# A state-space convolution beside a feed-forward block: late tiles transposed by VectorE, a three-row power table, the response's transform moved behind the next pair's run, and later marks

## The chip, the cores and the metric

The kernel runs on one core of a Trainium2 chip. The metric is device time in microseconds for one execution, lower is better. Engines are named as in the profile: PE is TensorE's matrix multiply, PEld its weight load, DVE is VectorE, ACT is ScalarE, POOL is GpSimd, SP is SyncE (here it only issues transfers). L-numbers are lines of the kernel before.

## The reference

All in float32, for one sequence of 2048 positions and 576 channels:

```python
x = A_u
xn = _layernorm(x, axis=-1)
return x + _A_ref(xn, ...) + _B_ref(xn, B_w1, B_w2)
```

`_B_ref` is the feed-forward block (FFN): `silu(xn @ w1) @ w2`, with 4608 hidden columns. `_A_ref` is a long convolution along the positions, one response per channel:

```python
dt = jnp.exp(log_dt)[:, None]
logdA, dB = dt * (A_re + 1j * A_im), dt * (B_re + 1j * B_im)
P = jnp.exp(logdA[:, :, None] * l[None, None, :])
K = jnp.einsum("dn,dnl,dn->dl", Cc, P, dB).real
...
y = irfft(rfft(pad(u)) * rfft(pad(K)))[:L] + u * Dskip
```

The response K of a channel is a sum over 128 states, at 2048 lags; generating it and the two transforms is what runs beside the FFN.

## The kernel before

**The main line of work** is the FFN (`ffn`). Positions are cut into 16 tiles of 128, four tiles make a block of 512, two blocks a half. For each half and each of nine chunks of hidden columns (four times 128), both blocks are worked on: `up` (L276) makes 128 hidden columns for 512 positions, 14 matmuls of 512 columns into `ph`; ACT applies silu (`gf`, L292) and rounds it to 12 bits (`gh`, L293), DVE takes the rest (`gl`, L294). `down` (L296) multiplies back, 24 matmuls of 288 columns for a tile into `po` (L309), and DVE adds to `acc` (L313). Every float32 operand is split in a high and a low part, and three products stand for one, so weights too are split when they arrive: w1r into w1h and w1l, w2r into w2h and w2l (L245 to L274). SP issues the weight loads.

**What is woven in** is a generator, `side` (L753). `weave` (L31) traces the FFN step by step (144 steps) and advances `side` when its next yield, a share of the FFN, has come; `marks = (0.13, 0.595, 0.822)` (L755) are the shares at which generation begins, the spectral stage begins, and that stage ends. From this trace a scheduler makes the fixed order in which each engine runs its instructions. `behind(x)` pins instructions after x on x's engine.

In order, `side` does this:

- `phase0` (L197) loads x, normalizes tiles in pairs (`norm`), and `put_xt` (L117) turns each tile on PE: four transposes of 128 by 128 into `pt` (L121), rounded by ACT into xh (L122), the rest by DVE into xl (L123), then the last 64 channels (L125 to L127). Tiles 0 to 7 go straight into the operands `xts` of the first half. Tiles 8 to 15 (the late tiles) are turned in the same way into `xt` and stored to `dxt`, both parts, in runs of 128 columns (L223); `next_xt` (L320) fetches xh, xl and x4 from there on POOL's queue when the last chunk of the first half begins. `dxn` keeps the normalized rows for the convolution.
- `natural` (L373) computes, per state and channel, the response's magnitude and phase and decay powers: `ex` holds the decay for 256, 64, 8 and 1 lags (L422), stored to `dexp`; `turned` (L387) transposes on PE into rhoT (magnitude) and phiT (phase).
- `kgen` (L490) generates the response in 36 runs of 16 channels, two runs to a pair. `load_bases` brings the decay bases of a pair, `powers` (L524) raises them to powers 0 to 7 in `pw`, four rows for a channel, and multiplies row 1 by rhoT into `al` (L536). Each run forms a phase table (`th`, `c65`; sines on ACT), a magnitude table in C (`al` times row 0, L562; row 2 times row 3, L566), and from them S and C (L577, L578). After the second run 64 small matmuls sum over the states into `kp` (L598), ACT copies it to `kt` (L605), eight matmuls with f1 (L613) make the first transform `z`, and ACT moves z into `stage` (L621), which every second pair SP stores to d1k (L626). The matmuls `pu` between them (L152, L153) are the same transform of the input (`spread`). kp, z, pu, pt and the spectral stage's pk and pb take turns in three PSUM banks (`pss`); po has three of its own (`ps2`), ph two.
- `spectral` (L632) works through 32 frequencies: loads, splits, products, the inverse of the inner transform into `pb`, ACT's copy `yo`, stored by POOL to d2 (L672).
- `tail` (L677) and the last chunk's `down` load d2 back as `ys` (L728; `conv_load`), and `add_conv` (L731) does the outer inverse in eight small matmuls `py` (L741) for a tile, added by DVE (L747). A ys needs all 32 frequencies.

Two things about the tile shapes matter: kp's matmuls use the array in strips of 32 columns (`tile_position=(0, 32 * q)`), z's in halves of 64 rows, py's in 64 by 32; all FFN matmuls use the whole array.

## Time and profile before

| | |
|---|---|
| median of 3 runs (lowest to highest) | 1133.25 us (1133.01 to 1133.71) |
| the profiled execution's own time | 1131.89 us |
| its span in the profile | 1130.1 us |
| PE busy, PEld busy | 1109.0 us, 999.9 us |
| DVE busy, ACT busy, POOL busy | 917.1, 709.0, 74.3 us |
| DVE busy from 180 to 660 us (generation) | 457.8 of 480 us |
| granted TensorE clock | 1.00 in all stretches up to 1110 us |
| bytes moved | 151.24 MB, 134 GB/s |

The span is the profile's, from the first to the last instruction; the execution's own time has 1.8 us more around it. A row of a group tells line, engine, operation, output and inputs, shape, count, then busy time and the mean of one in ns, then the engine's idle time just before it and what ended that. A row of the timeline gives start and length in us; PE's instructions overlap, so the length of one is not its price, and the step from start to start is. The ends of matmuls are modelled.

### The profile page before, as it was taken

To read this page: it belongs to the slowest core of one execution; us is meant where nothing else is said; L and a number is where in the kernel's file an instruction comes from. 1 tells how busy PE (TensorE), PEld (TensorE's weight loads), DVE (VectorE), ACT (ScalarE), POOL (GpSimd) and SP (SyncE) were. 2 spreads that over 40 slices of the span, in tenths; PEclk is the share of its full clock that TensorE was granted. 3 is DMA by queue.
4 is the path that set the end of the run, shared out by engine and by line. 5 is a ranking of instruction groups with operands and counts; after the bars stand their busy time and mean duration, and the time that the engine had idled before them with its cause. 6 is when DMAs were issued, how large, how long until landed. Compare 5 with 4: busy or idle time off the path is not lost.

```text
span 1130.1 us, 22882 instructions
## 1 busy us (share of the span) xinstructions
PE 1109.0 (98%) x9184; PEld 999.9 (88%) x9184; DVE 917.1 (81%) x1540; ACT 709.0 (63%) x1235; POOL 74.3 (7%) x130
## 2 busy tenths in 40 slices
PE   6999999999999999999999999999999999999998
PEld 5988889988889888898989999999999999998876
DVE  6699779999999999999999937788877878763433
ACT  4665355776777666667666637877777787752211
POOL 1010000000000000001000000000000000000210
PEclk9999999999999999999999999999999999999999
DMA  9345431334241424255954264554535536239661
GB/s 277 111 142 181 144 96 60 97 98 103 83 114 59 112 83 106 90 127 192 231 161 104 66 183 122 157 175 132 170 114 157 166 118 195 72 111 243 174 171 55
DMA packets 160458, 151.24 MB, mean 134 GB/s; under 512 B 87216, under 2 KB 127168, under 8 KB 159712
## 3 DMA queue, kind: packets, MB, share of 16 engines
q1 hardware_dynamic: 150128, 112.66, 36.2%
q0 software_dynamic: 9840, 36.24, 10.0%
q8 instruction: 72, 1.18, 0.4%
q10 hardware_dynamic: 384, 0.89, 0.3%
q14 instruction: 34, 0.28, 0.1%
HBM read 103.74 MB, written 46.08 MB: 133 GB/s over the span
## 4 chain that ended last, share of the span: by engine, by line
PE 65%; DVE 24%; DMA 5%; ACT 3%; issue 3%; POOL 0%; SPq 0%; DVEq 0%; ACTq 0%; POOLq 0%
PE po L309 28%; PE ph L284 23%; DVE acc L313 2%; DVE C L566 2%; PE pu L721 2%; PE pb L721 2%; PE pk L721 2%; DVE th L541 2%; DMA w2r<-in_B_w_dram 2%; DVE th L558 2%; DVE S L577 2%; PE ph L285 2%; PE ph L286 2%; DVE C L577 2%; DVE gl L294 2%
## 5 line engine op out<-in xcount | busy, mean ns | idle before, releaser
L309 PE MATMUL po<-w2h,gh 128*128 128x288 f32 x1152 | 338.5, 297 | 5.3 <-DVE acc L313 2.6
L309 PE MATMUL po<-w2l,gh 128*128 128x288 f32 x1152 | 337.1, 295 | 0.0
L309 PE MATMUL po<-w2h,gl 128*128 128x288 f32 x1152 | 335.3, 296 | 0.6 <-DVE gl L294 0.6
L309 PEld LDWEIGHTS po<-w2h,gh 128*128 128x128 f32 x1152 | 215.2, 188 | 16.8 <-DVE acc L313 4.9
L309 PEld LDWEIGHTS po<-w2l,gh 128*128 128x128 f32 x1152 | 215.5, 188 | 4.3
L309 PEld LDWEIGHTS po<-w2h,gl 128*128 128x128 f32 x1152 | 214.8, 188 | 3.0 <-issue 0.9
L284 PE MATMUL ph<-xh,w1h 128*128 128x512 f32 (+1 forms) x592 | 162.3, 390 | 0.5 <-ACT xh L122 0.5
L284 PE MATMUL ph<-xl,w1h 128*128 128x512 f32 (+1 forms) x592 | 162.1, 387 | 0.0
L284 PE MATMUL ph<-xh,w1l 128*128 128x512 f32 (+1 forms) x592 | 161.1, 385 | 0.0
L313 DVE TENSOR_TENSOR acc<-po,acc 128x288 f32<-128x288 f32 x288 | 126.9, 452 | 40.1 <-PE po L309 38.4
L292 ACT ACTIVATE gf<-ph 128x512 f32<-128x512 f32 (+1 forms) x148 | 86.6, 585 | 115.3 <-PE ph L286 106.1
L294 DVE TENSOR_TENSOR gl<-gf,gh 128x512 fp32r<-128x512 f32 (+1 forms) x148 | 99.6, 673 | 47.6 <-ACT gh L293 46.9
L284 PEld LDWEIGHTS ph<-xl,w1h 128*128 128x128 f32 x592 | 108.6, 190 | 20.2
L284 PEld LDWEIGHTS ph<-xh,w1l 128*128 128x128 f32 x592 | 108.0, 188 | 19.7
L284 PEld LDWEIGHTS ph<-xh,w1h 128*128 128x128 f32 x592 | 105.3, 190 | 19.0 <-issue 2.3
L293 ACT CAST gh<-gf 128x512 fp32r<-128x512 f32 (+1 forms) x148 | 89.7, 608 | 9.1 <-PE po L309 6.2
L559 ACT ACTIVATE c<-th 128x1040 f32<-128x1040 f32 x36 | 38.7, 1075 | 60.0 <-DVE th L558 59.9
L271 ACT CAST w2h<-w2r 128x576 fp32r<-128x576 f32 x72 | 46.7, 672 | 39.9 <-DMA w2r<-in_B_w_dram 23.4
L557 ACT ACTIVATE c<-th,magic 128x1040 f32<-128x1040 f32 x36 | 42.0, 1168 | 42.4 <-DVE C L578 36.5
L273 DVE TENSOR_TENSOR w2l<-w2r,w2h 128x576 fp32r<-128x576 f32 x72 | 53.4, 752 | 8.9 <-ACT w2h L271 8.9
L286 PE MATMUL ph<-x,w1l 128*128 128x512 f32 (+1 forms) x148 | 56.9, 385 | 0.0
L255 DVE TENSOR_TENSOR w1l<-w1r,w1h 128x640 fp32r<-128x640 f32 x72 | 56.7, 819 | 0.2
(186 smaller groups left out, 1847.2 us busy)
## 6 DMA issues: line engine op xcount, KB each, us to landing
w2r<-in_B_w_dram SPq DMA_DIRECT2D x72, 288.0 KB, 3.7
w1r<-in_B_w_dram SPq DMA_DIRECT2D x35, 512.0 KB, 3.8
d1u<-u POOLq DMA_DIRECT2D x32, 288.0 KB, 2.8
d1k<-stage SPq DMA_DIRECT2D x18, 512.0 KB, 7.2
ur<-d1u SPq DMA_DIRECT2D x32, 288.0 KB, 3.6
kr<-d1k SPq DMA_DIRECT2D x32, 288.0 KB, 2.8
d<-yo POOLq DMA_DIRECT2D x32, 288.0 KB, 3.6
ys<-d SPq DMA_DIRECT2D x32, 288.0 KB, 9.0
```

The lines of the kernel that those rows point to most:

```text
L255: pins["w1l"] = nc.vector.tensor_sub(l1, src, h1).ins
L271: pins["w2h"] = nc.scalar.copy(h2, r2).ins
L273: nc.vector.tensor_sub(l2, r2, h2)
L284: nc.tensor.matmul(ph, w[:, kt, :], v[:, kt, a:e], start=n + kt == 0, stop=False)
L286: pins["pe"] = nc.tensor.matmul(ph, l1[:, 4, :], x4[:, a:e], start=False, stop=True).ins
L292: nc.scalar.activation(gf, ph, AF.Silu)
L293: pins["gh"] = nc.scalar.copy(gh, gf).ins
L294: pins["gl"] = nc.vector.tensor_sub(gl, gf, gh).ins
L309: pins["pe"] = nc.tensor.matmul(po[:, :HD], G[blk, t][g][:, js], W2[half, c, t][w][:, hs], start=n == 0, stop=n == 3 * FT - 1).ins
L313: nc.vector.tensor_add(acc[j][:, hs], po[:, :HD], acc[j][:, hs])
L577: nc.vector.tensor_mul(ov3, t[:, :, 0:64].rearrange("n d (x y) -> n d x y", y=32), mv3)
L721: nc.tensor.matmul(dst, st, mv[:, hs], start=n == 0, stop=n == 3 * len(terms) - 1)
```

## The change

It has five parts, which touch each other little.

- **Late tiles turned by DVE.** For tiles 8 to 15 `put_xt` is no longer called. DVE's transpose, which turns each 32 by 32 block in place, is applied to the normalized tile as a whole, once for a tile, and eight transfers on SP for a pair put the blocks where they belong in a plain float32 `dxt` of 576 by 512, in runs of 32 columns (128 bytes). `next_xt` fetches the plain values into xl's place and the last 64 channels twice into a `gl` buffer, and the new `split_xt` rounds (ACT) and subtracts (DVE), 128 channels at a time, after the steps d3, u1 and u2 of the last chunk's blocks in the first half.
- **Three-row power table.** The decay for 64 lags leaves `ex`'s interleaved part and is kept apart; `pw` has three rows for a channel instead of four. The magnitude times its four powers of the 64-lag decay is computed once in `natural` (`wt`, three products of 576 columns), stored to `dmag`, and loaded for each pair as `wb` beside `eb`. The products `al` go, and the first magnitude product is done in two halves.
- **Transform behind the next pair's run.** z of a pair is traced after the kp matmuls of the following pair and pinned behind them, one after the other; `kt` has two buffers. The last pair's transform comes by itself at the end.
- **Later marks:** 0.14, 0.605 and 0.83.
- rhoT is no longer kept, since the magnitude goes to `wt`.

```diff
@@ -78,10 +78,11 @@
     d2 = dram.tile([32 * P, D], F32, name="d2")
-    dxt = [dram.tile([P, 9, 512], F32, name=f"dxt{b}") for b in range(2)]
+    dxt = [dram.tile([D, 512], F32, name=f"dxt{b}") for b in range(2)]
...
-    dexp = dram.tile([P, 4 * D], F32, name="dexp")
+    dexp = dram.tile([P, D, 3], F32, name="dexp")
+    dmag = dram.tile([P, D, 4], F32, name="dmag")
@@ -217,10 +218,16 @@
                 put_xt(xh[:, :, c], xl[:, :, c], x4[:, c], xn[:, i, :])
-            else:
-                xt = p0.tile([P, 9, P], F32R, tag="xt", name="xt", bufs=1)
-                put_xt(xt[:, 0:4, :], xt[:, 4:8, :], xt[:, 8, :], xn[:, i, :])
-                nc.sync.dma_start(dxt[b - 2][:, :, jj * P:(jj + 1) * P], xt.bitcast(F32))
+        if js[0] >= 8:
+            b, jj = divmod(js[0], 4)
+            tr = p0.tile([P, 2, D], F32, tag="tr", name="tr")
+            for i in range(2):
+                nc.vector.transpose(tr[:, i, :], xn[:, i, :])
+            for q in range(4):
+                cols = dxt[b - 2][:, jj * P:(jj + 2) * P].rearrange("(k r) (i q c) -> q r i k c", r=32, i=2, q=4)[q]
+                for i in range(2):
+                    nc.sync.dma_start(cols[:, i], tr[32 * q:32 * q + 32, i].rearrange("r (k c) -> r k c", c=32))
@@ -228,7 +235,7 @@
-        R1, R2 = {}, {}
+        R1, R2, R4 = {}, {}, {}
@@ -318,11 +325,24 @@
         def next_xt(b):
-            xt = new_xt(2 + b)
-            nc.gpsimd.dma_start(xt[0], dxt[b][:, 0:4, :])
-            nc.gpsimd.dma_start(xt[1], dxt[b][:, 4:8, :])
-            nc.gpsimd.dma_start(xt[2], dxt[b][:, 8, :])
-            xts[2 + b] = xt
+            xh, xl, x4 = xts[2 + b] = new_xt(2 + b)
+            nc.gpsimd.dma_start(xl.bitcast(F32), dxt[b][0:512].rearrange("(k p) t -> p k t", p=P))
+            r4 = gp.tile([P, 512], F32R, tag="gl", name="r4").bitcast(F32)
+            for h in range(2):
+                nc.gpsimd.dma_start(r4[64 * h:64 * h + 64], dxt[b][512:D])
+            R4[b] = r4
+        def split_xt(b, kt):
+            xh, xl, x4 = xts[2 + b]
+            with behind(pins["gh"]):
+                if kt < NKT:
+                    nc.scalar.copy(xh[:, kt], xl[:, kt].bitcast(F32))
+                    nc.vector.tensor_sub(xl[:, kt], xl[:, kt].bitcast(F32), xh[:, kt])
+                else:
+                    r4 = R4.pop(b)
+                    nc.scalar.copy(x4, r4)
+                    nc.vector.tensor_sub(x4[64:, :], r4[64:, :], x4[64:, :])
@@ -366,13 +386,16 @@
                     f(*new, t)
+                if half == 0 and c == NCH - 1:
+                    for kt in {"d3": (0, 1), "u1": (2, 3), "u2": (4,)}.get(step, ()):
+                        split_xt(b, kt)
...
-        fT, rhoT, phiT = (kf[n] for n in ("f", "rho", "phi"))
+        fT, phiT = kf["f"], kf["phi"]
@@ -419,8 +442,9 @@
         r = nat.tile([P, 4 * D], F32, tag="r", name="r")
-        for k, lag in enumerate((256.0, 64.0, 8.0, 1.0)):
-            nc.scalar.activation(ex.rearrange("n (d k) -> n k d", k=4)[:, k, :], lrT, AF.Tanh, scale=0.5 * lag)
+        for k, lag in enumerate((256.0, 8.0, 1.0, 64.0)):
+            dst = ex[:, :3 * D].rearrange("n (d k) -> n k d", k=3)[:, k, :] if k < 3 else ex[:, 3 * D:]
+            nc.scalar.activation(dst, lrT, AF.Tanh, scale=0.5 * lag)
@@ -433,7 +457,7 @@
             v.scalar_tensor_tensor(ex[:, c], ex[:, c], 1.0, r[:, c], op0=ALU.add, op1=ALU.mult)
-        nc.sync.dma_start(dexp, ex)
+        nc.sync.dma_start(dexp, ex[:, :3 * D].rearrange("n (d k) -> n d k", k=3))
@@ -484,11 +508,16 @@
         v.tensor_mul(t0, t0, rc)
-        turned(br, rhoT)
+        wt = nat.tile([P, D, 4], F32, tag="r", name="wt")
+        turned(br, wt[:, :, 0])
...
+        for k in range(3):
+            v.tensor_mul(wt[:, :, k + 1], wt[:, :, k], ex[:, 3 * D:])
+        nc.sync.dma_start(dmag, wt)
...
-        fT, rhoT, phiT = (kf[n] for n in ("f", "rho", "phi"))
+        fT, phiT = kf["f"], kf["phi"]
@@ -507,7 +536,7 @@
             nc.vector.memset(magic, MAGIC)
-            pw = kg.tile([P, 2, W, 4, 8], F32, name="pw")
+            pw = kg.tile([P, 2, W, 3, 8], F32, name="pw")
@@ -515,26 +544,28 @@
                 if i < NCK:
-                    bases.append(kg.tile([P, 2, W, 4], F32, tag="eb", name="eb", bufs=2))
-                    nc.sync.dma_start(bases[-1].rearrange("n g c k -> n g (c k)"),
-                                      dexp.rearrange("n (g r) -> n g r", g=2)[:, :, i * CH * 4:(i + 2) * CH * 4])
+                    eb = kg.tile([P, 2, 2, CH, 3], F32, tag="eb", name="eb", bufs=2)
+                    wb = kg.tile([P, 2, 2, CH, 4], F32, tag="wb", name="wb", bufs=2)
+                    for t, d in ((eb, dexp), (wb, dmag)):
+                        nc.sync.dma_start(t.rearrange("n g q c k -> n g (q c k)"),
+                                          d.rearrange("n (g r) k -> n g (r k)", g=2)[:, :, i * CH * d.shape[2]:
+                                                                                     (i + 2) * CH * d.shape[2]])
+                    bases.append((eb, wb))
...
-                al = kg.tile([P, 2, W, 4], F32, tag="al", name="al", bufs=2)
+                eb, wb = bases.pop(0)
...
-                               bases.pop(0).rearrange("n g (q c) k -> n q g (c k)", q=2))
+                               eb.rearrange("n g q c k -> n q g (c k)"))
...
-                R = 2 * W * 4
+                R = 2 * W * 3
...
-                for q in range(2):
-                    nc.vector.tensor_mul(split(al[:, q]), split(pw[:, q, :, 1, 0:4]), col(rhoT, i + q, 4))
-                return al
+                return wb
@@ -543,13 +574,37 @@
-            stage = None
+            def transform(kt, i, after):
+                nonlocal stage
+                z = [pss.tile([P, 512], F32, tag="pss", name="z") for _ in range(2)]
+                for eg in range(4):
+                    for h in (1, 0):
+                        rows = slice(64 * h, 64 * h + 64)
+                        with tc.high_priority(), behind(after):
+                            mm = nc.tensor.matmul(z[h][:, eg * P:(eg + 1) * P], kt[rows, eg * P:(eg + 1) * P], f1[rows],
+                                                  start=True, stop=True, tile_position=(64 * h, 0))
+                        after = mm.ins
+                r = (i - 1) % NRUN
+                if r == 0:
+                    stage = kg.tile([P, 64, NRUN * CH], F32, tag="stage", name="stage")
+                sv = stage[:, :, r * CH:(r + 2) * CH].rearrange("p k (e h c) -> p h e k c", h=2, c=2)
+                for h in range(2):
+                    nc.scalar.copy(sv[:, h], z[h].rearrange("p (e k c) -> p e k c", e=4, c=2))
+                if r == NRUN - 2:
+                    d0 = (i // NRUN) * NRUN * CH
+                    kv = d1k.rearrange("(k n) (g d) -> g n k d", n=64, g=2)
+                    for gp_ in range(2):
+                        nc.sync.dma_start(kv[gp_, :, :, d0:d0 + NRUN * CH], stage[gp_ * 64:(gp_ + 1) * 64])
+            stage = kt = None
...
-                pk, ak = pw[:, i % 2], al[:, i % 2]
+                pk, ak = pw[:, i % 2], al[:, :, i % 2]
@@ -559,14 +614,16 @@
                 nc.scalar.activation(c65, c65, AF.Sin, scale=-TWO_PI, bias=halfpi)
-                nc.vector.tensor_mul(
-                    mag[:, :, 0:32].rearrange("n d (x y) -> n d x y", y=4),
-                    pk[:, :, 0, :].unsqueeze(3).broadcast_to([P, W, 8, 4]),
-                    ak.unsqueeze(2).broadcast_to([P, W, 8, 4]))
+                for g in range(2):
+                    gs = slice(g * CH, (g + 1) * CH)
+                    nc.vector.tensor_mul(
+                        mag[:, gs, 0:32].rearrange("n d (x y) -> n d x y", y=4),
+                        pk[:, gs, 0, :].unsqueeze(3).broadcast_to([P, CH, 8, 4]),
+                        ak[:, g].unsqueeze(2).broadcast_to([P, CH, 8, 4]))
...
-                    pk[:, :, 2, :].unsqueeze(3).broadcast_to([P, W, 8, 8]),
-                    pk[:, :, 3, :].unsqueeze(2).broadcast_to([P, W, 8, 8]))
+                    pk[:, :, 1, :].unsqueeze(3).broadcast_to([P, W, 8, 8]),
+                    pk[:, :, 2, :].unsqueeze(2).broadcast_to([P, W, 8, 8]))
@@ -601,30 +658,12 @@
                 tabs = []
-                kt = kg.tile([P, 512], F32, tag="kt", name="kt")
+                if kt is not None:
+                    transform(kt, i - 2, mm.ins)
+                kt = kg.tile([P, 512], F32, tag="kt", name="kt", bufs=2)
...
-                z = [pss.tile([P, 512], F32, tag="pss", name="z") for _ in range(2)]
-                first = None
-                for eg in range(4):
-                    for h in (1, 0):
-                        rows = slice(64 * h, 64 * h + 64)
-                        with tc.high_priority(), behind(first):
-                            mm = nc.tensor.matmul(z[h][:, eg * P:(eg + 1) * P], kt[rows, eg * P:(eg + 1) * P], f1[rows],
-                                                  start=True, stop=True, tile_position=(64 * h, 0))
-                        first = first or mm.ins
-                r = (i - 1) % NRUN
-                if r == 0:
-                    stage = kg.tile([P, 64, NRUN * CH], F32, tag="stage", name="stage")
-                sv = stage[:, :, r * CH:(r + 2) * CH].rearrange("p k (e h c) -> p h e k c", h=2, c=2)
-                for h in range(2):
-                    nc.scalar.copy(sv[:, h], z[h].rearrange("p (e k c) -> p e k c", e=4, c=2))
-                if r == NRUN - 2:
-                    d0 = (i // NRUN) * NRUN * CH
-                    kv = d1k.rearrange("(k n) (g d) -> g n k d", n=64, g=2)
-                    for gp_ in range(2):
-                        nc.sync.dma_start(kv[gp_, :, :, d0:d0 + NRUN * CH], stage[gp_ * 64:(gp_ + 1) * 64])
...
+            transform(kt, NCK - 1, None)
@@ -752,7 +791,7 @@
         nonlocal s4, kl, yp, pa, tail_at
-        marks = (0.13, 0.595, 0.822)
+        marks = (0.14, 0.605, 0.83)
@@ -763,7 +802,7 @@
         with tc.tile_pool(name="kf", bufs=1) as kfp:
-            for n in ("f", "rho", "phi"):
+            for n in ("f", "phi"):
```

## The prediction

> **What bounds the kernel now.** I read the page's first two parts, then who waits for whom on TensorE (PE), then PE's instructions in order of time.
>
> ```profile
> PE 1109.0 (98%) x9184; PEld 999.9 (88%) x9184; DVE 917.1 (81%) x1540; ACT 709.0 (63%) x1235; POOL 74.3 (7%) x130
> ...
> PE   6999999999999999999999999999999999999998
> ...
> DVE  6699779999999999999999937788877878763433
> ...
> PEclk9999999999999999999999999999999999999999
> ```
>
> PE is busy in every slice at the full clock; VectorE (DVE) is full from slice 7 to 22 only, the generation of the response. So PE's own work sets the end, unless something makes it wait. The waits view says how much that is; its columns are the total in us, the number of waits, the longest.
>
> ```profile
> PE po L309 <- DVE acc L313: 2.6, 4, 1.4
> PE po L309 <- ACT w2h L271: 1.5, 1, 1.5
> PE po L309 <- ACT gh L293: 1.1, 2, 0.8
> PE pu L152 <- ACT stage L621: 0.4, 2, 0.2
> ```
>
> After the start-up, named waits are some 6 us. A microsecond taken from PE's list is therefore a microsecond of the end; one taken from DVE or ScalarE (ACT) counts only where PE waited. Starts show PE's prices: 0.131 us from one 288-column matmul to the next, 0.227 us for 512 columns. Small matmuls are dearer than their count: this is a transform (z) run, and the end of a kp run, on PE.
>
> ```profile
> 219.11 0.29 PE L309 MATMUL po<-w2l,gh 128*128 128x288 f32 x1
> 219.34 1.16 PE L613 MATMUL z<-f,kt 64*128 64x128 f32 x16
> 220.43 0.40 PE L152 MATMUL pu<-sp,s 128*128 128x288 f32 x1
> 220.67 0.29 PE L153 MATMUL pu<-sp,s 128*128 128x288 f32 x1
> ```
>
> ```profile
> 215.06 0.31 PE L598 MATMUL kp<-S 128*32 128x64 f32 x6
> 215.30 0.40 PE L309 MATMUL po<-w2h,gh 128*128 128x288 f32 x1
> 215.53 0.29 PE L309 MATMUL po<-w2l,gh 128*128 128x288 f32 x1
> ```
>
> Entering z takes 0.23 instead of 0.13 (0.09 lost). Leaving kp takes 0.15 from its last start (215.15, the six rows' end less the 0.22 of one), and the second matmul comes after 0.23, 0.10 late. Leaving z costs 0.20 and 0.11.
>
> **The change part by part.** The sum is made against the profiled execution, 1131.89 us (span 1130.1 and 1.8 around it), 1.4 under the median of 1133.25; I subtract the same from both. Where I speak of the new order, it is the order of the instructions in the two built programs.
>
> *Late tiles turned by DVE.* 40 PE transposes go (8 tiles x 5).
>
> ```profile
> 61.23 0.63 PE L284 MATMUL ph<-xl,w1h 128*128 128x512 f32 x2
> 61.70 0.60 PE L121 MATMUL pt<-ident,xj 128*128 128x128 f32 x4
> 62.14 0.27 PE L125 MATMUL pt<-ident,xj 128*64 128x128 f32 x1
> 62.25 0.60 PE L121 MATMUL pt<-ident,xj 128*128 128x128 f32 x4
> 62.60 0.70 PE L284 MATMUL ph<-xl,w1h 128*128 128x512 f32 x2
> ```
>
> Nine take 62.60 - 61.70 = 0.90 us, and the second matmul after them is 0.09 late: 0.11 each, 40 are **-4.4 us**, all on the path. ACT loses 8 x (0.58 + 0.25) and gains 8 copies of 0.61 and two like them (512 columns) at the half boundary: even, in its 37% of idle time. DVE loses 8 x (0.68 + 0.28) = 7.7 us, gains 8 turns of 576 columns, between 0.58 (L188) and 0.75 (L273) each, I take 0.68: 5.4, and 10 subtractions of 0.69 (L294's form) = 6.9 at 510 to 570 us. There DVE has no room: 97.8 of 100 us between 500 and 600. It can push generation back at no cost, but an acc addition (L313) queued behind two subtractions keeps a ps2 bank; three banks cover some 3 x 1.6 us of PE. I take **+0.5**, bounds 0 and 6.9 less the 2 us that the next part frees. The issues: SP gets 32 stores of 72 KB for 8 of 576 KB, POOL 3 loads for 3 per block.
>
> *Transform behind the next pair's run.* In the new order z follows kp's last matmul directly in 17 of 18 pairs, so 0.09 of entering and 0.15 + 0.10 of leaving go, and one switch from kp to z comes, which no row shows. Below: 0.01 (kp's own steps); above: 0.21, the longest step inside a z run. kp fills 128 rows by 32 columns, z 64 rows by 128, so I go by kp's exit to another shape, 0.15, and a little more: 0.17. 17 x (0.34 - 0.17) = **-2.9 us**, bounds -5.6 and -2.2. The Trainium skill, "TensorEngine Tiling (Array Packing)", Key Properties, says that changing the tiling mode drains the array: it speaks against a free switch, and kp's 0.15 agrees; without it the term would be -5.6.
> PE no longer waits for the copy kt: three z runs lost 0.20, 0.17 and 0.64 that way: **-1.0**. The last pair has no successor: its z stands apart, and split 1 + 7: **+0.4** (one more 0.09 + 0.20 + 0.11). What is late next: kp and both z hold all three pss banks, and the next pu now needs kt's copy within 1.2 to 3.7 us of FFN work. In the trace that copy ends 0.6 to 5.6 us after kp's end, z taking 1.1 of it: **+0.5**, bounds 0 and 17 x 0.7.
>
> *Three-row power table.* DVE, per pair of runs:
>
> ```profile
> L562 DVE TENSOR_TENSOR C<-pw,al 128x512 f32<-128x512 f32 x36 | 24.7, 685 | 0.7 <-PE kp L598 0.7
> L533 DVE TENSOR_TENSOR pw<-pw 128x256 f32<-128x256 f32 x18 | 11.3, 626 | 0.0
> L534 DVE TENSOR_TENSOR pw<-pw 128x384 f32<-128x384 f32 x18 | 9.9, 553 | 0.1
> L532 DVE TENSOR_TENSOR pw<-pw 128x128 f32<-128x128 f32 x18 | 7.8, 431 | 0.1
> L536 DVE TENSOR_TENSOR al<-pw,rhoT 128x64 f32<-128x64 f32 x36 | 6.4, 218 | 0.0
> ```
>
> The three power rows lose a quarter of their columns: of 1.61 us some 0.36, as 0.06 of each is fixed. Two al products go: 0.44. L562 splits in halves, 0.39 each for 0.685: +0.10 twice. Net -0.6 a pair, -11 us over 18, and +2.3 once for three 576-column products (0.75). All of it is DVE time, none on PE. It thins the queue in which PE's 5 us of generation waits (180 to 660 us) arose: DVE was 458 of 480 us busy, 2% goes. I take **-1.0**, bounds -5 and 0. Its extra loads (wb, 64 KB like eb's, 2.2 us to landing) are asked a pair ahead.
>
> *Later marks.* They move the spectral stage back against the FFN, and its end is what the last convolution needs. From the last pb to the first py, PE has 110 FFN matmuls now (20.9 us); in the new order 69: 19 x 0.227 + 50 x 0.131 = 10.9 us. The chain that must fit in between:
>
> ```profile
> 1012.90 0.54 POOL L672 DMA_DIRECT2D d<-yo  x1 [5.54 <-ACT yo L671]
> ```
> ```profile
> 1016.57 1.28 SPq L728 DMA_DIRECT2D ys<-d  x2
> 1017.90 0.60 SPq L683 DMA_DIRECT2D r<-dr  x1
> ```
>
> The last pb starts at 1011.36. By the landing records its output is in memory at 1016.4, the two halves of ys 0 land at 1020.7 and 1022.1 (10.7 us after the pb), those of ys 1 at 1025.6 and 1026.9 (15.5). So the first py just fits; the next add_conv, which the new order puts 1.1 us of FFN after it (at 13.0 with the py run's 0.74), waits 2.5 us. Two weight loads shared the engines with this chain and now stand earlier: I take **+2.0**, bounds 0 and 10. One more add_conv is split in two runs: **+0.7** (a lone run of 8 costs 0.71, a double one 0.74). PE takes its list in order, so everything behind a late py shifts.
>
> Sum: -4.4 + 0.5 - 2.9 - 1.0 + 0.4 + 0.5 - 1.0 + 2.0 + 0.7 = **-5.2 us**: 1126.7 for a profiled run, **1128.0** by the median.
>
> **Rivals.**
> (a) *The stores clog SP, and it gets slower.* From 60 to 150 us SP issues, ahead of w1r and w2r, eight stores a pair (0.4 to 0.56 each, the rows of L224 and L223) for two of 0.56: +2.1 to +3.4 us, four times. Against: ACT took its w2h waits (14 us in generation alone) mostly without PE noticing. For: PE's one wait for w2h, 1.5 us at 132, lies in this stretch. It decides where a w2r lands later than PE's next block of po begins. If every delay reached PE: 4 x 3.4 = 13.6, 1141.6; half of them: 1134.8. Rows of 128 bytes are slow in this trace: stage to d1k, 512 KB, 7.2 us to landing against 4.1 for dxt's 576 KB in rows of 512. The Trainium skill, "DMA: Bandwidth & Descriptors", gives 512 bytes as the least for full rate; the two rows agree. 10%.
> (b) *The tail wait eats the gain.* ys loads land 9.0 us after issue at the median, 12.8 at most; only the first two took 4.1 and 4.8. At 9.0 the first py waits 5.9 + 9.0 - 11.0 = 3.9, the second add_conv 2.9 more: 6.8 for my 2.0, which gives 1132.8. For: the old slack of 10 us is gone. Against: nothing queues before the first two. 14%.
> (c) *DVE's relief ends all generation waits and the tail fits:* -4.0 and -2.0 more: 1122.0. 10%.
> (d) The parts do what they say but fewer than a third of the gains reach the end, because DVE, not PE, sets the pace of 180 to 660 us: -1.5, 1131.8. Against: 5 us of waits in 480. 6%.
>
> **How the numbers follow.** Forecast 60%, 1125 to 1130.5; the four rivals above. A run of this kernel can be told from no change beyond 0.2%, 2.3 us: under 1131.0 is faster. Faster: 60 + 10 and a little of (b) and (d), 73%; same 17%; slower, (a), 10%. The range 1122.5 to 1133.5 takes in the bounds of the two least sure terms, the tail and generation waits, and leaves out most of (a) and half of (c).
>
> **What would show it.** No pt after 40 us; z right behind kp with a step of 0.15 to 0.21 us; L562's successor at 0.39; PE's waits for acc, gl and stage under 4 us from 180 to 660; a wait at the second py run near 1020 us of about 2 us. Waits of po for w2h between 60 and 150 us above 3 us would mean (a); a first py that waits means (b).

## The result, and the profile after

Slower, where faster was foretold: 1140.57 us at the median of five runs (1139.17 to 1140.97), against 1133.01 for the kernel before in the same comparison; the ratio is 1.006, its 95% interval 1.0045 to 1.0076. The forecast was 1128.0, the range ended at 1133.5. The profiled execution took 1140.97 us, its span is 1139.2, 9.1 more than before. The kernel before is less steady than its three executions in the table: in the comparisons below it took from 1129.5 to 1139.1 us, those executions with a mean granted clock of 0.995 took 1137.2 or more, those with 1.000 at most 1134.8. L-numbers are now those of the changed kernel, some 7 higher in the FFN (po is L316, acc L320, w1h L260, w1l L262) and up to 40 higher behind it (py L780, ys L767).

The page of the changed kernel, its first two parts:

```profile
PE 1108.2 (97%) x9144; PEld 1001.8 (88%) x9144; DVE 918.1 (81%) x1545; ACT 708.0 (62%) x1229; POOL 79.3 (7%) x130
...
PE   6999899999999999999999999999999999999798
...
DVE  6699799999999999999999847878778787773333
...
PEclk9999999999999999999999999999999999999899
```

PE has 40 instructions less and is as busy as before; near the end its row falls to 7, and so, new, does the granted clock's to 8. The waits of PE say more (total in us, times, longest):

```profile
PE po L316 <- DVE acc L320: 10.6, 2, 6.9
...
PE pu L153 <- ACT kt L664: 2.3, 1, 2.3
...
PE py L780 <- DMA ys<-d: 0.2, 1, 0.2
```

Three waits carry it: 3.7 us for acc at 120, 2.3 for kt at 521, 6.9 for acc at 1057. The py that I had feared for waits 0.2.

**A ledger.** PE takes its list in order, so its time over the plain price of its large matmuls (on average 0.229, 0.132 and 0.120 us from start to start for 512, 288 and 256 columns) can be booked: small runs with what entering and leaving them costs, and all other delay, by stretch. In us, from the starts in both traces:

| | before | after | change | foretold |
|---|---|---|---|---|
| pt and ptk | 14.6 | 10.3 | -4.3 | -4.4 |
| kp and z | 63.4 | 60.0 | -3.4 | -2.5 |
| py | 15.1 | 15.9 | +0.8 | +0.7 |
| delay from 60 to 180 us | 2.5 | 7.4 | +4.9 | 0 (rival a: up to 13.6) |
| delay from 180 to 720 us | 6.3 | 7.4 | +1.1 | -1.0 |
| delay after 1020 us | 0.0 | 9.9 | +9.9 | +2.0 |

With 0.1 elsewhere this makes the span's 9.1. So the gains on PE came, and were lost in two places. (-2.5 is z's -2.9 and +0.4; -1.0 is the sum of +0.5, -1.0, +0.5 and -1.0. Some 0.6 of kp and z's -3.4 is a wait for kt inside one z run of the kernel before, at 547 us; it belongs to the second of these four terms.)

**The tail, 1057 us.** Read from PE backwards: PE, DVE, ACT and SP of the changed kernel, start and length first.

```profile
1057.54 0.29 PE L316 MATMUL po<-w2h,gl 128*128 128x288 f32 x1
1064.75 0.61 PE L316 MATMUL po<-w2h,gh 128*128 128x288 f32 x1 [6.91 <-DVE acc L320]
1065.15 0.44 PE L316 MATMUL po<-w2l,gh 128*128 128x288 f32 x1
1065.39 0.44 PE L316 MATMUL po<-w2h,gl 128*128 128x288 f32 x1
```
```profile
1062.77 1.56 DVE L262 TENSOR_TENSOR w1l<-w1r,w1h 128x640 fp32r<-128x640 f32 x2 [9.22 <-ACT w1h L260]
1064.24 0.45 DVE L320 TENSOR_TENSOR acc<-po,acc 128x288 f32<-128x288 f32 x1
```
```profile
1062.01 1.35 ACT L260 CAST w1h<-w1r 128x640 fp32r<-128x640 f32 x2 [9.33 <-DMA w1r<-in_B_w_dram]
```
```profile
1033.89 1.28 SPq L767 DMA_DIRECT2D ys<-d  x2
...
1039.27 3.66 SPq L767 DMA_DIRECT2D ys<-d  x4
...
1045.07 0.38 SPq L247 DMA_DIRECT2D w1r<-in_B_w_dram  x1
1047.46 1.86 SPq L248 DMA_DIRECT2D w1r<-in_B_w_dram  x1
1050.47 0.49 SPq L249 DMA_DIRECT2D w1r<-in_B_w_dram  x1
```

PE waits for an addition that DVE could have made at once; but DVE takes its list in order too, and ahead of it stands the split of the next chunk's weights, which waits for ACT, which waits for a load. SP asked for that load behind ten transfers of ys and three of r, and those waited for the last two stores to d2 (SP waited 16.3 us for them, 2.6 before). The last store went out at 1031.28, before at 1012.90; w1r was asked at 1045.07 and landed in up to 16.3 us. In the kernel before it was asked at 1036.38 and landed in 5.0 at most:

```profile
1036.38 0.37 SPq L240 DMA_DIRECT2D w1r<-in_B_w_dram  x1
```

DVE's row also shows what a wait costs that is not its own: with no addition made, three banks of po fill (36 matmuls, the last at 1057.54), and PE stops. And behind the wait a matmul of 288 columns takes 0.24 from start to start, not 0.13.

**At 120 us**, SP and DVE of the changed kernel:

```profile
110.80 5.03 SPq L230 DMA_DIRECT2D dxt<-tr  x8
115.87 1.91 SPq L164 DMA_DIRECT2D xj<-in_A_u_dram  x4
```
```profile
117.71 1.22 DVE L516 TENSOR_TENSOR wt<-wt,ex 128x576 f32<-128x576 f32 x1
118.85 0.94 DVE L506 TENSOR_TENSOR t<-t,are 96x768 f32<-96x768 f32 x1
120.94 1.54 DVE L180 BATCH_NORM_STATS2 st<-xj 128x6 f32<-128x288 f32 x4 [1.16 <-DMA xj<-in_A_u_dram]
122.40 1.15 DVE L516 TENSOR_TENSOR wt<-wt,ex 128x576 f32<-128x576 f32 x1
123.46 0.45 DVE L320 TENSOR_TENSOR acc<-po,acc 128x288 f32<-128x288 f32 x1
```

The eight small stores hold the next pair's x loads on SP for 5 us; DVE reaches the statistics of that pair, waits for x, and the addition that PE needs comes 5.7 us after the one before. Of these 5.7 DVE is idle for x in 1.2 only; the rest is work that its list puts between the two additions (two wt products, another product and the statistics). This is rival (a), with the loads of x in the place of w2r; the sign that the prediction gave for (a), waits of po for w2h above 3 us, did not come (0.8).

**At 521 us** ACT copies kt (L664) at 523.28, after two of the new xh copies (1.13 us) and a phase table (1.06), and pu waits 2.3 us for it:

```profile
521.27 1.13 ACT L340 CAST xh<-xl 128x512 fp32r<-128x512 f32 x2
522.31 1.06 ACT L614 ACTIVATE c<-th 128x1040 f32<-128x1040 f32 x1
523.28 0.56 ACT L664 COPY kt<-kp 128x512 f32<-128x512 f32 x1
```

The splits are not all of it. Without these two copies kt would come some 1.0 us sooner; ahead of them in ACT's list stand the split of w1 (1.35 us) and a phase table that had waited 2.5 us for DVE.

### The profile page after: what moved, and what is told of

Same layout as the page of the kernel before. It is cut to its first block, busy times and chain, and to the rows that moved or that the text cites. A ratio compares the mean times of both kernels' runs of the same rounds, so it can differ in the third digit from the quotient of the medians.

```text
span 1139.2 us, 22884 instructions
## 1 busy us (share of the span) xinstructions
PE 1108.2 (97%) x9144; PEld 1001.8 (88%) x9144; DVE 918.1 (81%) x1545; ACT 708.0 (62%) x1229; POOL 79.3 (7%) x130
## 4 chain that ended last, share of the span: by engine, by line
PE 55%; DVE 22%; DMA 8%; issue 7%; ACT 5%; SPq 2%; POOL 1%; DVEq 0%; ACTq 0%; POOLq 0%
PE po L316 23%; PE ph L291 19%; DMA w1r<-in_B_w_dram 2%; DVE acc L320 2%; PE pu L760 2%; PE pb L760 2%; PE pk L760 2%; DVE th L572 2%; DVE S L634 2%; DVE gl L301 2%; DVE C L623 2%; DVE th L613 2%; DVE w1l L262 2%; PE ph L292 2%; PE ph L293 2%
## 5 line engine op out<-in xcount | busy, mean ns | idle before, releaser
L316 PE MATMUL po<-w2h,gh 128*128 128x288 f32 x1152 | 339.5, 299 | 12.3 <-DVE acc L320 10.6
L316 PE MATMUL po<-w2l,gh 128*128 128x288 f32 x1152 | 339.4, 297 | 0.4 <-DVE w2l L280 0.4
L316 PE MATMUL po<-w2h,gl 128*128 128x288 f32 x1152 | 338.0, 298 | 0.6 <-DVE gl L301 0.6
L316 PEld LDWEIGHTS po<-w2h,gh 128*128 128x128 f32 x1152 | 217.3, 190 | 24.2 <-DVE acc L320 12.0
L316 PEld LDWEIGHTS po<-w2l,gh 128*128 128x128 f32 x1152 | 217.8, 190 | 5.4 <-DVE w2l L280 0.6
L316 PEld LDWEIGHTS po<-w2h,gl 128*128 128x128 f32 x1152 | 217.1, 190 | 3.1 <-DVE gl L301 1.2
L320 DVE TENSOR_TENSOR acc<-po,acc 128x288 f32<-128x288 f32 x288 | 126.5, 451 | 51.9 <-PE po L316 50.3
L262 DVE TENSOR_TENSOR w1l<-w1r,w1h 128x640 fp32r<-128x640 f32 x72 | 57.2, 819 | 9.5 <-ACT w1h L260 9.2
```

The costliest lines, as they stand in the source:

```text
L262: pins["w1l"] = nc.vector.tensor_sub(l1, src, h1).ins
L316: pins["pe"] = nc.tensor.matmul(po[:, :HD], G[blk, t][g][:, js], W2[half, c, t][w][:, hs], start=n == 0, stop=n == 3 * FT - 1).ins
L320: nc.vector.tensor_add(acc[j][:, hs], po[:, :HD], acc[j][:, hs])
```

## The experiments

All are compared with the kernel before on the same chip. A distance is given for each below: TensorE's work, at plain prices and in the built order, from the last pb of the spectral stage to the end. It is 104 us in the kernel before and 84 in the changed one.

**1. The marks.** In the changed kernel:

```diff
-        marks = (0.14, 0.605, 0.83)
+        marks = (0.13, 0.595, 0.822)
```

> The changed kernel with the marks of before (0.13, 0.595, 0.822). In the built order the last pb comes 5.8 us of TensorE work earlier than in the changed kernel (969.1 for 974.9), so the first ys load may start 5.6 us earlier. Theory A (the late end of the spectral stage holds SP, SP's late w1r load makes DVE, and so TensorE, wait 7.1 us at 1057, and the half clock behind it costs 2.6 more): the wait shrinks to about 1.3 us, no half clock, so 1140.6 - 8.4 = 1132 us. Theory B (the marks do little; the tail wait comes from crowded DMA engines, whatever the order): the wait stays above 5 us and the time stays at 1139 to 1141. The waits at 120 and 521 us lie ahead of the tail; A expects both to stay, within 1 us.

Measured (e1): 1130.8 us, ratio 0.9981 (0.9967 to 0.9994); distance 90. No delay after 1020 us but 1.3 in the py runs. The wait at 120 us stayed, 3.1 of PE's 3.5 for acc. Theory A. The converse, the new marks in the kernel before (the same two lines exchanged):

> The kernel before with the marks of the change alone (0.14, 0.605, 0.83). In the built order the last pb moves from 104 us to 84 us ahead of the end, and from the first ys load to the last split of w1 only 16 us of TensorE work are left, as in the changed kernel (35 before). Theory A (marks alone make the tail wait): a wait of about 7 us for acc near 1060 us and a half clock behind it, 9 us more than before: 1142 us. Rival (the tail wait needs the other parts too): within 2 us of before, 1133 to 1135.

Measured (e2): 1141.53, ratio 1.007 (1.0049 to 1.0091); distance 84; 8.6 us of delay in the tail, acc 2.9 and ys 1.5 of it named:

```profile
PE po L309 <- DVE acc L313: 6.6, 5, 2.9
...
PE py L741 <- DMA ys<-d: 1.5, 1, 1.5
```

So the new marks are enough for the tail's loss, and without them it is nearly gone.

**2. What is late in the tail.**

```diff
-            eng = nc.gpsimd if first and t == 0 else nc.sync
+            eng = nc.gpsimd if first and t == 0 or (half, c, t) == (1, NCH - 1, 2) else nc.sync
```

> The changed kernel with one load moved from SP's queue to POOL's: the last chunk's second w1r (three transfers, 640 KB in all), which stands on SP behind ten ys loads and three r loads. Theory A1 (it is late because of its place in SP's queue): it is asked at about 1042.5, when its buffer is free, and lands in 5 to 8 us, before ACT wants it at 1052.7; no wait at 1057, no half clock: 1140.6 - 9.5 = 1131 us. Theory A2 (it is late because the DMA engines are full with ys and r transfers from 1035 to 1062, whatever the queue): it lands only near 1058, the wait is 3 us or more, and the time is 1135 to 1140.

Measured (e3): 1138.7, ratio 1.0046 (1.0029 to 1.0062). The wait at 1057 is gone, and another has come, with its half clock:

```profile
1075.88 0.39 PE L293 MATMUL ph<-x,w1l 128*128 128x512 f32 x1
1081.36 1.18 PE L780 MATMUL py<-ys,s 64*32 64x288 f32 x8 [5.10 <-DMA ys<-d]
```

w1r, asked at 1040.6, landed in 10 us and was 0.3 late: A1 for this load. But ys loads came late in its stead, at 1081. In this run the DMA engines were busy without a gap from 1035 to 1085 us (share 1.07 on average, 260 GB/s), while the kernel before had a slack stretch there (share 0.27 from 1045 to 1055). So neither theory was whole. As the runs stand together, what has to be loaded behind the last stores to d2 is a train that fills the DMA engines; its late start makes something late, and the order of asking decides which load.

```diff
-        for j in range(8):
-            for f in (conv_load, load_r0)[:2 - j % 2]:
-                steps.append((at, f, j))
-                at += tail_at[1]
+        for f, j in [(load_r0, j) for j in range(0, 8, 2)] + [(conv_load, j) for j in range(8)]:
+            steps.append((at, f, j))
+            at += tail_at[1]
```

> The changed kernel, its marks kept, with the four r loads of the last convolution (2.36 MB, which need nothing of the spectral stage) ahead of the ys loads on SP's queue, and not between them. SP sat idle there from 1017 to 1033.9, waiting for the last store to d2. Theory A (the tail is a train of transfers, some 7 MB of ys, r and w1, that starts with the last d2 store and runs its engines full; a start 18 us late makes whatever stands last in it late): four loads of 576 KB leave the train, 10 us of it at the 230 GB/s of that stretch; w1r lands some 9 us earlier, no wait above 1 us at 1057 and no half clock: 1140.6 - 9 = 1131.5 us, within 2. Rival (the memory that r0 takes is freed only with the last pb, so the loads start as late as now, or ys 0 is late behind them and the first py waits): under 3 us of gain, 1138 to 1141.

Measured (e5): 1135.73, ratio 1.0023 (1.0003 to 1.0042), half of the gain. The r loads went out at 1031.19, not at 1017: they too waited for the last store to d2, at 1028.59. That their memory is that of the spectral stage is the likely reason; it was not tried with other memory.

**3. Late tiles.** First the changed kernel with its late tiles on PE again (the diff's parts for `normed`, `next_xt` and `split_xt` reversed):

```diff
-            for i in range(2):
-                nc.vector.transpose(tr[:, i, :], xn[:, i, :])
...
+                put_xt(xt[:, 0:4, :], xt[:, 4:8, :], xt[:, 8, :], xn[:, i, :])
+                nc.sync.dma_start(dxt[b - 2][:, :, jj * P:(jj + 1) * P], xt.bitcast(F32))
```

> The changed kernel with the late tiles turned on TensorE again, as before (40 transposes, eight 576 KB stores for 32 small ones, no splits by ACT and DVE at the half boundary); all else is that of the change. Theory C (the turn by DVE brings the waits at 120 us, 3.9 us, and 521 us, 2.4 us, each with a half clock of 3.4 us behind it): transposes +4.0, these waits and their half clocks -7 to -9, tail wait as it was: 1136 to 1138 us. Rival (the waits there come from the other parts, the wt products at 117 to 123 us and the kt copy's place): they stay and the time is 1144 to 1145.

Measured (e4): 1136.89, ratio 1.0027 (1.0011 to 1.0043). The wait at 120 us is gone (delay from 60 to 180 us 1.2), transposes +4.3 as expected, but in place of kt's wait at 521 there is one of 3.3 us at 504, behind a late w2r load, also with half clock; the tail lost 8.1 (distance 88). Theory C for 120 us; for 521 the run does not decide, since the order changed with the tiles. That the time fell within its 1136 to 1138 is partly luck: the tail gained 2.6 and the generation lost 3. Then that part alone, in the kernel before (the same lines exchanged):

> The kernel before with the late tiles turned by DVE and nothing else of the change. Theory C (the turn saves 4 us of transposes and pays with a wait at 120 us of some 3 us, with a half clock behind it, for eight stores a pair on SP hold the next xj loads, and DVE's statistics wait for these ahead of acc): 1133 - 4 + 4 = 1133 us, with a wait over 2 us between 95 and 135 us. Rival (the wait at 120 us needs the wt products of the power table): no wait above 1.7 us there and 1129 us.

Measured (e6): 1130.21, ratio 0.9975 (0.9958 to 0.9993). DVE in its trace, without any wt product:

```profile
117.55 0.95 DVE L504 TENSOR_TENSOR t<-t,are 96x768 f32<-96x768 f32 x1
120.38 1.54 DVE L179 BATCH_NORM_STATS2 st<-xj 128x6 f32<-128x288 f32 x4 [1.88 <-DMA xj<-in_A_u_dram]
...
123.16 0.45 DVE L319 TENSOR_TENSOR acc<-po,acc 128x288 f32<-128x288 f32 x1
```

PE waited 3.6 us for this acc. The wt products are not needed for the wait. DVE was idle for x in 1.9 of the 5.6 us between the two additions; the rest is its own work in between. The transposes' 4.7 us came, and no half clock (below says why).

**4. The stores on another queue.** One word, in three kernels: the changed one, the changed one with the old marks, and the kernel before with DVE's turn alone:

```diff
-                    nc.sync.dma_start(cols[:, i], tr[32 * q:32 * q + 32, i].rearrange("r (k c) -> r k c", c=32))
+                    nc.gpsimd.dma_start(cols[:, i], tr[32 * q:32 * q + 32, i].rearrange("r (k c) -> r k c", c=32))
```

> The changed kernel, its marks kept, with the 32 small stores of the turned tiles on POOL's queue. In the built order the last pb stands 4 us of TensorE work earlier than in the changed kernel (970.8 for 974.9). The wait at 120 us (3.9 us) and its half clock (1.7) should go, as with the marks of before: -5. The tail, 4 us earlier, should lose some 4 of its 9.5: 1140.6 - 9 = 1131.5 us. If the tail wait comes with the marks whatever the start, only the 5 go: 1135.5.

Measured (e10): 1127.37, ratio 0.9948 (0.9928 to 0.9967): 13.2 us under the changed kernel. SP now asks for x 2.8 us after it has stored the pair before to dxn, not 5.7:

```profile
104.60 0.33 SPq L231 DMA_DIRECT2D dxn<-xj  x1
107.42 2.11 SPq L164 DMA_DIRECT2D xj<-in_A_u_dram  x4
```

Delay from 60 to 180 us fell from 7.4 to 1.1. The last store to d2 came 10 us sooner (1021.17). Six of these are the waits that went; they shift PE's whole list, the tail with it, and give it no slack. The other four are distance, 88 for 84, since the scheduler's order changes with the queue too. At the tail's steep place that was enough: 2.8 us of delay there, for 10.7. DVE's order changes too. Between the two additions at this place stand one product and the statistics, where the changed kernel had three products and the statistics, and DVE still waits 0.7 us for x. So the stores on SP bring the wait and the move takes it away, but how much of that is the earlier landing of x, and how much the order built around it, these runs don't separate.

> The changed kernel with the marks of before and the 32 small stores of the turned tiles issued on POOL's queue, not SP's. Theory C (those stores hold xj and weight loads back on SP; DVE waits for xj ahead of its acc additions): the wait at 120 us (3.3 us, and 3.4 of half clock worth, in the run with old marks) goes under 1 us: about 4 us off that run's time, 1127 us. Rival (the clump of DVE work at 117 to 123 us, three wt products and the phase's own, makes the wait, whatever SP does): the wait stays above 2 us and the time at 1130 to 1131.

Measured (e8): 1126.34, ratio 0.9946 (0.9929 to 0.9963). Theory C: the delay from 60 to 180 us went from 9.3 to 2.6. The wt products stand later here, so the run does not test them at their old place; e6 does. The old marks add nothing that can be measured to what the queue gave with the new ones.

> The kernel before with the late tiles turned by DVE and their 32 stores on POOL's queue, nothing else. Theory C: the prediction's -4.4 + 0.5 for the tiles comes out in full once SP is free of the stores: the wait near 120 us goes, 1132.5 - 4.5 = 1128 us or less. Rival (the 4 us that TensorE saves are given back in waits between 180 and 660 us, for DVE and ACT set the pace there): no better than with the stores on SP, 1130 us.

Measured (e11): 1121.9, ratio 0.9893 (0.9865 to 0.9922), better than theory C: delay of 0.3 us from 60 to 180 (2.5 before) and 3.9 from 180 to 720 (6.3). So by the ledger some 4.5 us of the gain are the transposes and 4.6 are waits that the kernel before had. This beats both kernels, by 10.4 and some 19 us.

**5. Table and transform.** The table alone in the kernel before, and with the transform (the second kt fits in memory only with the smaller table); each is its part of the diff:

```diff
-            pw = kg.tile([P, 2, W, 4, 8], F32, name="pw")
+            pw = kg.tile([P, 2, W, 3, 8], F32, name="pw")
...
+                if kt is not None:
+                    transform(kt, i - 2, mm.ins)
+                kt = kg.tile([P, 512], F32, tag="kt", name="kt", bufs=2)
```

The first is the table's (e9), both are e7's; e12 has the table's and the tiles of e11.

> The kernel before with the three-row power table alone. TensorE's order is that of before. By the prediction: 11 us of DVE time less in 180 to 660 us, of which TensorE keeps 1.0 (bounds 0 and 5): 1131 to 1132 us. The pair of table and transform together gave 1125.3; if the table makes most of it (relief of DVE ends the waits): 1128 or less, and the transform is worth the rest, under 3; if the transform makes most of it: 1131 or more.

Measured (e9): 1128.84, ratio 0.9957 (0.9941 to 0.9972): -3.5, between the two cases. Its trace does not show the relief that was named: in the profiled execution, the slowest of ten (1130.77), the delay from 180 to 720 us is about 1.3 us more than before, and that from 60 to 180 is 2.3 less. Where the gain arises stays open.

> The kernel before with the three-row power table and the transform behind the next pair's run (the transform alone finds no memory for its second kt; the table makes the room), late tiles and marks as before. By the prediction's terms: z -2.9, waits for kt -1.0, last split +0.4, pu's waits +0.5, generation -1.0, tail nearly as before (the last pb 4 us of TensorE later): -4, 1129 us. By the trace of the changed kernel, where entering z lost 1.9 us in all and leaving it 0.2: -2 for z and -1 to -5 for the waits in 180 to 660 us: 1126 to 1130 us. Rival (the kt copy behind other ACT work holds pu in every pair, or the wt products hold acc near 120 us): 1132 to 1134.

Measured (e7): 1125.3, ratio 0.9935 (0.9913 to 0.9958): -6.6 at the median, more than the prediction's -4. By the ratios the transform's share is 2.5 us, with intervals that overlap; by the ledger kp and z give the same 3.4 us as in the changed kernel.

> The kernel before with the late tiles turned by DVE (stores on POOL's queue) and the three-row power table, the transform and the marks as before. The table alone gave -3.5, these tiles alone -10.4, all three parts with the old marks and these stores -6. If the gains add: 1118.5 us. If the transform is what spoils the sum (its kt copies hold pu, 3 us in that run): 1118 to 1120. If the table does (DVE is no longer what TensorE waits for once the tiles are out of SP's way, and the built order puts the last pb 88 us ahead of the end, 104 with the tiles alone): some 2 us of tail wait, nothing gained, 1122 to 1127.

Measured (e12): 1127.01, ratio 0.9955 (0.9942 to 0.9969): the last case: worse than the tiles alone by 5 us at the medians. By the ledger 4.1 in the tail (distance 88 again, 104 with the tiles alone), 2.4 up to 180 us, 1.1 in kp runs, less 1.0 from 180 to 720.

**6. Is it the distance?** Earlier marks in the changed kernel (e13), in that of e8 (e14) and in that of e12 (e15):

```diff
-        marks = (0.14, 0.605, 0.83)
+        marks = (0.13, 0.585, 0.812)
```

> The changed kernel, stores on SP, with the marks 10 thousandths earlier than before's (0.13, 0.585, 0.812): the last pb stands 98 us of TensorE work ahead of the end (104 in the kernel before, 90 with the old marks, 84 in the changed kernel). It parts the two causes that hang together so far. If the tail alone counts for the marks and the stores cost their own 5 us near 120 us: tail costs as in the kernel before, the wait near 120 us stays: some 1 us under the run with the old marks, 1129 to 1130 us. If the stores' cost is mostly by the way of the tail: under 1127 us. If a denser generation gives the gain back in waits between 180 and 600 us: 1131 or more.

Measured (e13): 1134.64, ratio 1.0019 (1.0001 to 1.0036).

> All three parts of the change, the stores on POOL's queue, and marks 10 thousandths earlier than before's: the last pb 100 us ahead of the end (95 with the old marks, 1126.3 us). If the distance alone spoiled the sum, it lost 0.8 us in the tail there: 1125.5 us. If a denser generation brings waits: 1127 or more. That it should reach 1120 would mean that something else than the tail went with the marks.

Measured (e14): 1130.95, ratio 0.9974 (0.9955 to 0.9994).

> Tiles by DVE with the stores on POOL and the power table, transform as before, marks 10 thousandths earlier: the last pb 104 us ahead of the end, as with the tiles alone (1121.9 us), for 88 with the old marks (1127.0 us). The tail of that run cost 4 us more than the kernel before's, and two waits at 118 and 147 us 2.5 more. If the distance spoiled the table's gain: 1127 - 4 = 1123 us, or 1121 with what the table saves between 180 and 660 us. If the table costs by itself (its wt products on DVE near 120 us): 1124 to 1127.

Measured (e15): 1129.6, ratio 0.9976 (0.9961 to 0.999). All three lost, by 2 to 5 us against the same kernel with the marks of before (e1, e8, e12), though the tail did what the distance says. e13 and e14 came out in the cases that named a denser generation; e15 lay above all of its cases. Tail delay by distance, from the ledgers of seventeen profiled executions (py over 15.05 us, and delay after 1020):

| distance, us | 100 to 104 | 95 to 98 | 90 | 88 | 84 |
|---|---|---|---|---|---|
| tail delay, us | 0 (6 kernels) | 0.8 (3) | 1.3 | 2.8, 4.1, 8.1 | 6.8 (r first), 8.6, 10.4 (w1r by POOL), 10.7 |

It is free down to some 95 (the 0.8 there is the price of one more py run, not a wait) and steep under 90, where the same distance of 88 gave from 2.8 to 8.1: the distance is not the only cause. The rest is not explained by it. Delay from 180 to 720 us lies anywhere between 2.9 and 10.5 us in these executions: 7.7 rose to 9.6 in e14, and 2.9 to 6.5 in e15. Which wait arises there depends on how each pair falls against the FFN's steps, and every edit shifts that. One execution for each kernel does not say what of it is luck: e1's profiled execution is the slowest of its twelve (1133.79), e13's the fastest of its ten (1132.80), and by these two e13 lost nothing, where the medians say 3.8. Why the parts' gains do not add stays open.

## Why the prediction was wrong, step by step

- **Late tiles, -4.4:** measured -4.3. The price of a transpose and its neighbours was right. With it came a cost that stood under rival (a) at 10%, and not in the sum: +4.9 up to 180 us. I named SP's eight stores and looked for a late w2r; it was the loads of x behind them, and through DVE's order, more than through DVE's idle time for x (1.2 us), the additions. On POOL's queue the same part alone gave -10.4.
- **z, -2.9 and +0.4:** measured -3.4 with kp and z together, or about -2.8 without the wait inside a z run. All 17 steps from kp to z took 0.148 to 0.150 us, kp's own exit price; I had taken 0.17. The switch is not free, as the Trainium skill, "TensorEngine Tiling (Array Packing)", Key Properties, says of a changed tiling mode; here it costs what leaving kp costs anyway. In the changed kernel:

```profile
234.95 0.31 PE L655 MATMUL kp<-S 128*32 128x64 f32 x6
235.19 1.16 PE L586 MATMUL z<-f,kt 64*128 64x128 f32 x16
236.28 0.40 PE L316 MATMUL po<-w2h,gh 128*128 128x288 f32 x1
```

- **Waits of the generation** (+0.5, -1.0, +0.5, -1.0): +1.1 for -1.0. Of the 6.3 us of before all but some 2 went, as rival (c) had it, and 5.2 came between 507 and 528 us: the waits of 0.9 and 2.4 by the starts, and the half clock behind. The first came behind a late w2r load (ACT waited 3.9 us for it). The second is the wait of pu for kt that the prediction had as its +0.5: the mechanism was foretold, but it came once and with half clock behind it, 4.1 us in all. There the new splits stood in ACT's way, for 1.0 of it, where I had looked for DVE's.
- **Later marks, +2.0, bounds 0 and 10: the step that failed.** Measured +9.9. I asked when py's own data would be there, and it was: 0.2 us. But "Two weight loads shared the engines with this chain and now stand earlier" left out the third, the last chunk's second w1r, which stands behind the ys loads on the same queue. With SP's start 17 us later it was what came last. The price went over PE's three banks, DVE's order and ACT, none of which I had followed from SP's queue on. The 9.9 lies just inside the term's own bounds; but the stated range did not take these bounds in, as it says: with +10 for the tail the sum is 1136.0, and the range ends at 1133.5.
- **py, +0.7:** +0.8.
- **The rivals:** (a), 1141.6, lay near the result by a mechanism of which only a part held; (b) had the right place, the tail, which was the larger part and more than its price, but not the way: its sign was a first py that waits, and py waited 0.2. That (a)'s 1141.6 is so near the result is luck. I had weighed them as alternatives, each against a forecast in which the other did not happen. They are not exclusive, and their prices add: 4.9 and 9.9 are more than all that the change saves. Nor are they independent: e10's one word takes most of both away, the second by way of the built order. The five parts do not touch each other little, as the description of the change says: they meet in SP's queue and in the lists of DVE and ACT.

## What to carry to other kernels

Where several engines take their lists in order, a late transfer does not stop its own reader alone: ask of each queue what stands behind the waiting transfer, and of each reader what stands behind it. A slack that is given away (here 104 us to 84) costs next to nothing until it is gone and then much at once (no wait in the tail down to 95 us, 6.8 to 10.7 at 84), so measure how far it goes, and don't price it by the first consumer only. Many small stores belong on a queue on which nothing urgent waits; here that one word was worth more than the change.

## What the runs showed of the hardware

**The clock falls by windows.** In its profiled execution the kernel before kept full clock from its start-up to its last microsecond; the changed one lost it three times in between. PE in six stretches about the tail's wait, in the changed kernel (stretch, length, PE busy and matmuls, granted clock, DMA share, GB/s):

```profile
1053.10:1056.50 3.40, 3.40 (x38) 1.00 1.04 357
1056.50:1059.90 3.40, 1.33 (x11) 1.00 1.10 264
1060.00:1063.30 3.30, 0.00 (x0) 0.50 0.96 190
1063.40:1066.70 3.30, 1.95 (x8) 0.50 0.14 24
1066.80:1070.10 3.30, 3.30 (x15) 0.50 0.95 286
1070.30:1073.60 3.30, 3.30 (x37) 1.00 1.05 313
```

In the fifth stretch PE makes 15 matmuls, 0.24 us apart; 25 would fit at 0.131. PE works on at half speed for a whole window after this wait is over, and a full window loses it 1.7 us (half of 3.4). In every trace the starts of half clock lie whole multiples of 3.413 us apart (124.69, 524.05 and 1059.94 us here: 117 and 157 of them). Of the windows of this grid that began at full clock, by the starts of matmuls and in all traces after 40 us, all 17 with 2.26 us or more without work were followed by half clock, and none with 2.05 or less; one of about 2.1, which also held a lone run of py, was followed by it too. So 2.4 us can be enough (521 us), and 3.7 are not where they fall in two windows, 2.05 and 1.79 (e6, at 120 us). The Trainium skill, "TensorE: Matmul & The Clock Gate", Part 1, states a free-running window of 3413 ns; the grid agrees. The Trainium skill, "TensorE: Matmul & The Clock Gate", HAM oscillation, has gaps over some 3.4 us as what to avoid; by these runs two thirds of a window (2.26 of 3.41 us) are enough.

**A load behind a train of others.** With ys and r loads under way at 190 to 360 GB/s, the three transfers of the late w1r (640 KB) took 14.2 us at the median to land, and 4.2 in the kernel before. By the landing records the ten ys loads, the three r loads and w1r landed in the order in which SP had asked for them, from 1037.7 to 1061.9 us; on POOL's queue (e3) the same w1r took 9.8 us, with the DMA engines as full.
